# 128 bytes of padding in SBUF ahead of the K and V buffers of a decode kernel

## The chip, the cores and the metric

One core of a Trainium2 chip. The metric is the device time of one execution in microseconds, as a median over the runs of a kernel. All runs told here are of the fast kind; a kernel's runs agree within about 0.5%, most within 0.3%. Each ran beside runs of the kernel before on the same chip, so a kernel is compared by its ratio to the runs beside it.

## The reference, cut to what matters

One decode step for 8 sequences: layer norm, Q projection, attention of 32 query heads over the last 2048 positions of an 8-head KV cache, output projection, residual, then a small gated-shift block whose shifts are zero for one token, so that only its MLP (W3, GELU, W4) is left.

```python
W = min(4096, max(256, Sk // 4))                 # 2048
q = (x @ wq).reshape(B, Sq, Hq, Dh)...           # 8 x 1 x 512 by 512 x 4096
k = jnp.repeat(k_cache[:, :, Sk - W:, :], rep, axis=1)
v = jnp.repeat(v_cache[:, :, Sk - W:, :], rep, axis=1)
p = softmax(einsum(q, k) * Dh ** -0.5);  o = einsum(p, v) @ wo
...
h2 = gelu(layernorm(x1) @ w3) @ w4
```

K and V are 33.5 MB each in bf16, wq and wo 4 MB each, w3 and w4 1.8 MB each: 79 MB are read, and little is computed on them.

## The kernel before

Tiles are allocated one after another inside a partition, in the order of the code. The ones that matter (cut; the remarks are added here):

```python
wbig = sb([128, KC * H * DH], dt.bfloat16, "wbig")     # wq, later wo
qblk = sb([128, B, G, H], dt.bfloat16, "qblk")
knat = sb([128, NK, NC * DH], dt.bfloat16, "knat")     # 15 K slots of 4096 bytes; later w3, w4
...
vnat = sb([128, NV, NC * DH], dt.bfloat16, "vnat")     # 16 V slots of 4096 bytes
kT_sb = sb([128, NKT, W], dt.bfloat16, "kT_sb")        # K transposed, written by ScalarE and VectorE
```

SyncE issues all transfers into one queue: x, wq, then K slots with V five items behind, then wo, w3, w4. Each K or V transfer is 512 KB, one contiguous row of 4096 bytes per partition:

```python
e.dma_start(
    knat[:, ks, :].rearrange("p (c d) -> p c d", c=NC),
    A_k_cache[b, g, W0:SK, :].rearrange("(p c) d -> p c d", c=NC),
).then_inc(sem_k[ks], 16)
```

TensorE transposes each K slot into PSUM, ScalarE and VectorE move the halves to kT_sb, and TensorE makes QK and, once per sequence after the softmax, PV.

Of the kernel before, what the change touches and what calls it, by code (L numbers as in the profile page):

```python
# [6 lines left out]
dt = mybir.dt  # L7
# [26 lines left out]
def bass_sequential_preLN__sliding_block_cached__mixer_s_mlp__decode_kernel(  # L34
# [23 lines left out]
    with es:  # L58
        sb = lambda shape, dtype, name: es.enter_context(nc.sbuf_tensor(name, shape, dtype))
# [22 lines left out]

        qblk = sb([128, B, G, H], dt.bfloat16, "qblk")

        knat = sb([128, NK, NC * DH], dt.bfloat16, "knat")
        W3_SLOT0, W4_SLOT0 = 4, 8
        SLOT_E = NC * DH
# [667 lines left out]
```

## Time and profile before

| | before |
|---|---|
| median time | 207.4 us |
| span in the profile | 205.6 us |
| flow in the middle of the stream | 408 GB/s |
| PE busy, granted clock | 78%, 0.82 |
| first and second part of W4 land at | 199.98 and 201.91 us |

The flow of the DMA queue is the row to watch: the queue is full from the second slice of 40 to the 38th, and the flow is flat from the fourth to the 33rd. The prediction shows the lines. That is the first of W4's two parts (the semaphore updates in the trace show both, at 199.98 and 201.91), and TensorE waits once more for the second:

```profile
201.95 0.95 PEld L689 LDWEIGHTS b<-knat,gT 128*8 128x8 bf16 x12 [0.46 <-DMA knat<-in_B_w_dram]
```

### The profile page before, as it was taken

To read this page: it belongs to the slowest core of one execution; us is meant where nothing else is said; L and a number is where in the kernel's file an instruction comes from. 1 tells how busy PE (TensorE), PEld (TensorE's weight loads), DVE (VectorE), ACT (ScalarE), POOL (GpSimd) and SP (SyncE) were. 2 spreads that over 40 slices of the span, in tenths; PEclk is the share of its full clock that TensorE was granted. 3 is DMA by queue.
4 is the path that set the end of the run, shared out by engine and by line. 5 is a ranking of instruction groups with operands and counts; after the bars stand their busy time and mean duration, and the time that the engine had idled before them with its cause. 6 is when DMAs were issued, how large, how long until landed. Compare 5 with 4: busy or idle time off the path is not lost.

```text
span 205.6 us, 6282 instructions
## 1 busy us (share of the span) xinstructions
PE 161.1 (78%) x2744; PEld 123.5 (60%) x2744; DVE 83.4 (41%) x197; ACT 81.8 (40%) x101; POOL 3.0 (1%) x13
## 2 busy tenths in 40 slices
PE   1039957799779977995899699698996698775645
PEld 0039745487548754873688468575884576565542
DVE  5103534624562356234454444347345253351120
ACT  3203846514641464145523561157145341350040
POOL 5000000000000000000000000000000000000000
PEclk9999997975997599769696969579969588885556
DMA  6999999999999999999999999999999999999980
GB/s 206 440 388 416 409 408 410 409 408 407 405 411 408 407 410 409 406 409 410 406 410 406 408 409 410 407 406 408 409 406 408 410 410 381 356 393 340 398 305 22
DMA packets 24250, 79.59 MB, mean 387 GB/s; under 512 B 2192, under 2 KB 6304, under 8 KB 24096
## 3 DMA queue, kind: packets, MB, share of 16 engines
q1 hardware_dynamic: 24224, 79.19, 97.9%
q8 instruction: 22, 0.36, 0.7%
q14 instruction: 4, 0.03, 0.0%
HBM read 79.18 MB, written 0.01 MB: 385 GB/s over the span
## 4 chain that ended last, share of the span: by engine, by line
DMA 54%; SPq 24%; PE 18%; issue 2%; DVE 0%
DMA knat<-in_A_k_cache_dram 48%; SPq L239 12%; PE kT_ps L385 10%; SPq L249 7%; DMA knat<-in_B_w_dram 6%; SPq L259 4%; PE misc L523 3%; PE S_ps L415 2%; PE b L689 2%; SPq L277 1%; PE b L470 0%; PE misc L443 0%; PE b L504 0%; PE misc L475 0%; DVE out_sb L699 0%
## 5 line engine op out<-in xcount | busy, mean ns | idle before, releaser
L396 ACT ACTIVATE kT_sb<-kT_ps 128x1024 bf16<-128x1024 bf16 x64 | 65.4, 1023 | 87.7 <-PE kT_ps L385 87.6
L385 PE MATMUL kT_ps<-ident_b,knat 128*128 128x128 bf16 x1024 | 84.6, 249 | 19.6 <-DMA knat<-in_A_k_cache_dram 18.6
L385 PEld LDWEIGHTS kT_ps<-ident_b,knat 128*128 128x128 bf16 x1024 | 72.4, 113 | 36.9 <-DMA knat<-in_A_k_cache_dram 27.8
L403 DVE COPY kT_sb<-kT_ps 128x1024 bf16<-128x1024 bf16 x64 | 44.2, 691 | 61.9 <-PE kT_ps L385 61.9
L523 PE MATMUL misc<-pT_sb,vnat 128*128 128x4 bf16 x1024 | 29.0, 165 | 3.1 <-issue 1.6
L523 PEld LDWEIGHTS misc<-pT_sb,vnat 128*128 128x128 bf16 x1024 | 27.4, 98 | 6.6 <-issue 4.2
L415 PE MATMUL S_ps<-kT_sb,qblk 128*32 128x512 bf16 x256 | 29.0, 446 | 0.3 <-DVE kT_sb L403 0.3
L415 PEld LDWEIGHTS S_ps<-kT_sb,qblk 128*32 128x32 bf16 x256 | 6.6, 95 | 8.8 <-issue 3.3
L357 PE MATMUL S_ps<-xlnT,wbig 128*128 128x8 bf16 x128 | 3.6, 168 | 6.5 <-DMA wbig<-in_A_wq_dram 6.5
L436 ACT ACTIVATE P_sb<-S_ps,negmcol 128x512 bf16<-128x512 f32 x8 | 5.5, 687 | 7.2 <-DVE negmcol L428 7.2
L533 DVE TENSOR_TENSOR prod_sb<-misc,w_sb 128x128 f32<-128x128 f32 x8 | 2.3, 292 | 14.7 <-PE misc L523 14.7
L509 DVE COPY w_sb<-b 128x128 f32<-128x128 f32 x8 | 2.3, 292 | 13.5 <-PE b L504 13.5
L357 PEld LDWEIGHTS S_ps<-xlnT,wbig 128*128 128x128 bf16 x128 | 3.5, 104 | 6.5 <-issue 6.5
L426 DVE TENSOR_REDUCE mcol<-S_ps 128x1 f32<-128x512 f32 x8 | 5.5, 682 | 0.6 <-PE S_ps L415 0.6
L581 ACT ACTIVATE std<-var,eps_t 128x8 f32<-128x8 f32 x1 | 0.3, 301 | 12.4 <-DVE var L632 12.4
L373 DVE TENSOR_SCALAR qblk<-S_ps 128x32 bf16<-128x32 f32 x8 | 0.9, 182 | 9.8 <-PE S_ps L357 9.8
L504 PE MATMUL b<-w_row,ones_row 1*128 1x128 f32 x16 | 4.7, 385 | 0.0
L460 ACT ACTIVATE a_row<-d_row 1x128 f32<-1x128 f32 x8 | 2.5, 306 | 5.7 <-DVE d_row L453 5.7
L443 PE MATMUL misc<-ident_f,mcol 128*1 128x128 f32 x16 | 3.8, 328 | 1.0 <-DVE negmcol L428 1.0
L599 PE MATMUL S_ps<-oT_all,wbig 128*128 128x8 bf16 x128 | 3.7, 168 | 0.7 <-DMA wbig<-in_A_wo_dram 0.7
L599 PEld LDWEIGHTS S_ps<-oT_all,wbig 128*128 128x128 bf16 x128 | 3.6, 104 | 0.8 <-DMA wbig<-in_A_wo_dram 0.8
L659 PE MATMUL misc<-uT,knat 128*128 128x8 bf16 x56 | 1.7, 168 | 2.7 <-DMA knat<-in_B_w_dram 2.7
(78 smaller groups left out, 70.0 us busy)
## 6 DMA issues: line engine op xcount, KB each, us to landing
knat<-in_A_k_cache_dram SPq DMA_DIRECT2D x64, 512.0 KB, 15.6
vnat<-in_A_v_cache_dram SPq DMA_DIRECT2D x64, 512.0 KB, 15.8
wbig<-in_A_wq_dram SPq DMA_DIRECT2D x1, 4096.0 KB, 12.3
wbig<-in_A_wo_dram SPq DMA_DIRECT2D x1, 2048.0 KB, 19.9
knat<-in_B_w_dram SPq DMA_DIRECT2D x1, 1792.0 KB, 12.3
wbig<-in_A_wo_dram SPq DMA_DIRECT2D x1, 1024.0 KB, 12.3
wbig<-in_A_wo_dram SPq DMA_DIRECT2D x2, 512.0 KB, 11.2
knat<-in_B_w_dram SPq DMA_DIRECT2D x1, 1024.0 KB, 12.8
```

Source lines behind the costliest of these rows:

```text
L239: e.dma_start(vnat[:, vs, :].rearrange("p (c d) -> p c d", c=NC), A_v_cache[b, g, W0:SK, :].rearrange("(p c) d -> p c d", c=NC),).then_inc ...
L249: e.dma_start(knat[:, ks, :].rearrange("p (c d) -> p c d", c=NC), A_k_cache[b, g, W0:SK, :].rearrange("(p c) d -> p c d", c=NC),).then_inc ...
L259: e.dma_start(wo_v[:, h0:h1, :], A_wo[h0 * 128:h1 * 128, :].rearrange("(h p) n -> p h n", p=128)).then_inc(sem_wo[j], 16)
L357: ins = e.matmul(S_ps[:, 0, h * B:(h + 1) * B], wq_v[:, kc, h * DH:(h + 1) * DH], xlnT[:, kc * B:(kc + 1) * B], start=(kc == 0), stop=(kc ...
L385: ins = e.matmul(buf[:, c * 128:(c + 1) * 128], knat[:, ks, c * DH:(c + 1) * DH], ident_b[:, :], is_transpose=True)
L396: e.activation(kT_sb[:, i % NKT, 0:W // 2], kT_ps[i % 2][:, 0:W // 2], ACT.Copy).then_inc(sem_Elo, 1)
L403: e.tensor_copy(kT_sb[:, i % NKT, W // 2:W], kT_ps[i % 2][:, W // 2:W]).then_inc(sem_Ehi, 1)
L415: ins = e.matmul(S_ps[32 * q:32 * (q + 1), b % 2, :], qblk[:, b, g, :], kT_sb[:, i % NKT, 512 * q:512 * (q + 1)], start=(g == 0), stop=(g ...
L426: ins = e.tensor_reduce(mcol[:, j:j + 1], S_ps[:, j, :], AX.X, ALU.max)
L436: e.activation(P_sb[:, j, :], S_ps[:, j, :], ACT.Exp, bias=negmcol[:, j:j + 1], scale=1.0, accum_out=lcol[:, j:j + 1]).then_inc(sem_exp, 1)
L523: ins = e.matmul(misc[:, OT4.start + q * H + R * g:OT4.start + q * H + R * (g + 1)], vnat[:, vs, c * DH:(c + 1) * DH], pT_sb[:, b % 2, c, ...
L599: ins = e.matmul(hT_ps[:, k * B:(k + 1) * B], wo_v[:, h, k * 128:(k + 1) * 128], oT_all[:, h, :], start=False, stop=(h == H - 1), skip_gro ...
```

## The change

The intent is that the rows written by the transfers of K, V and the weights in the same buffer begin on a boundary of 512 bytes inside the partition. The tile itself is used by nothing.

```diff
         qblk = sb([128, B, G, H], dt.bfloat16, "qblk")
 
+        pad = sb([128, 128], dt.uint8, "pad")
         knat = sb([128, NK, NC * DH], dt.bfloat16, "knat")
```

## The prediction

> **What bounds the kernel now.** I read the 40 slices first, because they say whether one resource is full from end to end. Slices are 205.6 / 40 = 5.14 us.

> ```profile
> PE   1039957799779977995899699698996698775645
> ...
> PEclk9999997975997599769696969579969588885556
> DMA  6999999999999999999999999999999999999980
> GB/s 206 440 388 416 409 408 410 409 408 407 405 411 408 407 410 409 406 409 410 406 410 406 408 409 410 407 406 408 409 406 408 410 410 381 356 393 340 398 305 22
> DMA packets 24250, 79.59 MB, mean 387 GB/s; under 512 B 2192, under 2 KB 6304, under 8 KB 24096
> q1 hardware_dynamic: 24224, 79.19, 97.9%
> ```

> The DMA row is 9 from the second slice to the 38th, and from slice 4 to slice 33 the rate is flat at 405 to 416 GB/s: a queue that never empties and runs at a rate of its own. PE is high but not full. The stretches by time say the same with numbers (columns: length, busy time of PE, PEld, DVE, ACT, POOL, then clock, DMA share, GB/s):

> ```profile
> 40.00:60.00 20.00, 17.42 (x297) 13.56 (x296) 9.12 (x21) 9.14 (x11) 0.00 (x0) 0.83 1.02 407
> 60.00:80.00 20.00, 17.33 (x296) 13.36 (x294) 9.02 (x22) 8.70 (x12) 0.00 (x0) 0.83 1.03 409
> 120.00:140.00 20.00, 18.37 (x296) 13.91 (x294) 8.82 (x20) 8.03 (x9) 0.00 (x0) 0.78 1.03 408
> 140.00:160.00 20.00, 16.54 (x292) 12.64 (x289) 10.10 (x23) 9.37 (x12) 0.00 (x0) 0.91 1.03 408
> ```

> PE has 8 to 17% to spare at the granted clock while the DMA engines have none. Then the chain that ended last, to see what sets the end:

> ```profile
> DMA 54%; SPq 24%; PE 18%; issue 2%; DVE 0%
> DMA knat<-in_A_k_cache_dram 48%; SPq L239 12%; PE kT_ps L385 10%; SPq L249 7%; DMA knat<-in_B_w_dram 6%; SPq L259 4%; PE misc L523 3%; PE S_ps L415 2%; PE b L689 2%; SPq L277 1%; PE b L470 0%; PE misc L443 0%; PE b L504 0%; PE misc L475 0%; DVE out_sb L699 0%
> ```

> and its last pieces in order of time:

> ```profile
> 185.09 2.06 SPq L277
> 187.19 12.79 DMA knat<-in_B_w_dram
> 199.98 0.14 issue
> 200.12 3.30 PE b L689 x28
> 203.44 0.41 DVE out_sb L699
> ```

> The last transfer, W4, lands at 199.98, and only some 5.6 us of work follows. So the time is: all bytes through one full DMA queue, plus a short tail. Whatever shortens or lengthens each packet moves the end; nothing else in this diff could.

> **Where the packets go.** K and V are 128 transfers with one row of 4096 bytes per partition: 16384 packets, 1024 on each of 16 engines. The allocation table of the compiled kernel before gives the starts inside a partition: wbig 20864, knat 57728, vnat 119168, each 384 above a multiple of 512, that is 128 above a multiple of 256. Slots are 4096 bytes and W3's rows 3584 (7 times 512), so every packet of K, V, W3 and W4 starts at that offset. x_sb starts at 18624 (192 above a multiple of 256), out_sb at 212736 (a multiple of 256).

> [...]

> [...] Flow of 408 GB/s over 16 engines is 25.5 GB/s each, and 4096 bytes at that take 160.6 ns[...]. The packet records give the commonest durations by size: 1024 bytes 46 ns, 2048 84, 3584 140, 4096 159, 32768 1213. [...] a fixed 8.3 ns[...], per packet whatever its size. That is all an alignment could hope to take away[...].

> **The change part by part.** It adds one tile that nothing reads or writes: no instruction, wait or transfer is added or removed. It moves knat and everything allocated after it by 128 bytes: knat and vnat start at multiples of 512. wbig lies ahead of the pad, so wq and wo keep their offset, although the words of the change speak of weights: of these only W3 and W4, which live in knat, move. out_sb goes from a multiple of 256 to 128 above one. The end of the allocation, 213760 plus 128, stays within the partition.

> Packets that move, per engine: K and V 1024, W3 512/16 = 32, W4 896/16 = 56, together 1112. Each ns off a packet is therefore 1.11 us off the full queue, 0.54% of the time. Two per cent needs 4.15/1.11 = 3.7 ns of the 8.3.

> Is any of the 8.3 ns due to the offset? There are two comparisons inside this trace. First, x's 1024 byte rows land in SBUF at 192 above a boundary, and the output's 1024 byte rows leave SBUF and land in HBM with both ends on one; both come one to an engine, with no traffic of their own behind them. The commonest duration is 44 ns for x (6 of 8 packets) and 44 ns for the output (4 of 8, the others longer). [...] Second, the 4 byte completion writes, which cross no boundary, take 9 ns[...]. Both say that the 8.3 ns belong to the packet, not to its address. I choose **no saving** as the main case: 0 x 1112 = 0 us, time 207.4. TensorE, ScalarE and VectorE read and write the moved tiles at offsets that were multiples of 64 bytes before and still are; I count nothing for them.

> **The rivals.**
> 1. [...] A misaligned 4096 byte row touches 17 blocks of 256, not 16; [...] Against it: it leaves nothing for the packet's own overhead, and the output's aligned 1024 bytes should take 37.6 ns, not 44. Worth 9.4 x 1.11 = 10.5 us of queue. PE, 104 to 110 us busy in 120 of the stretch 40 to 160, would then have little slack, and in the half-clock spells (120 to 140, where the chain was PE's) it would stop the slot releases; I estimate 70 to 90% realised: 198 to 200 us.
> 2. [...] Worth 5.2 us: about 202.2, or 203 if PE keeps a little.
> 3. [...] 1.3 us, 206.1, which counts as the same. The 2 ns between x's isolated 44 ns and wo's 46 leave room for this much.
> 4. The write side is not the limit at all, and the read of HBM, whose rows are aligned before and after, sets the pace. Then even a real saving on the write is hidden: 207.4.
> 5. Slower: only by chance of SBUF placement. Nothing in the profile speaks for it; the output's misaligned read is 8 packets.

> **Range and chances.** I give the main case with rivals 3 and 4 about 77%, rivals 1 and 2 together 22% (most of it to 2 or a part of it), slower 1%. The three times before span 0.3%. The middle of this is a little under the time before: 207.0 us, range 204.0 to 208.2.

> **What would show it.** Right: the flat rate stays at 407 to 410 GB/s, the commonest 4096 byte packet stays at 159 ns, W4 lands near 200 and PE keeps its idle time on K. If the flow rises to 420 and the packet falls to about 155 ns, rival 2 holds; near 435 and 150 ns, rival 1. A control lies inside the run: wo's 1024 byte packets do not move and should keep 46 ns in all cases. Flow up but the time not, with longer waits of the DMA queue for PE and a rate with dips, would mean that PE took the bound over. My step most likely to fail is the inference from isolated packets of x and the output to packets back to back in a full queue.

The fixed 8.3 ns of a packet and the sizes of the first two rivals follow from the commonest durations listed there, of the kernel before. From 46 ns at 1024 bytes to 1213 ns at 32768 a packet grows by (1213 - 46) / 124 = 9.41 ns for each 256 bytes, and 46 - 4 x 9.41 leaves 8.4 ns at no bytes; both are estimates. Rival 1 puts one more piece of 9.41 ns on each row that starts off a multiple of 256: 17 x 9.41 = 160.0 ns, close to the 160.6 of the flow, and 5, 9, 15 and 129 such pieces are 47, 85, 141 and 1214 ns, close to the records too, so the sizes alone cannot choose between it and a fixed cost. Rival 2 puts on it the 128 bytes ahead of the row's start, 4.7 ns. Rival 3 is a small cost per row; its 1.3 us were the author's estimate. No run had shown yet that a row pays for any of them.

## The result, and the profile after

| | before | after |
|---|---|---|
| median time, us | 207.4 (207.33 to 207.88) | 202.89 (202.86 to 202.97) |
| ratio | 1 | 0.9778, interval 0.9762 to 0.9795 |

A ratio is the mean time of one kernel's fast runs over that of the other's fast runs of the same rounds, so it is not quite the ratio of the two medians. The kernel is 2.2% faster: faster, where the prediction had put 77% on the same.

The slices of the kernel after, in the same rows as before:

```profile
PE   2029985999679977995899779797998499785655
DMA  6999999999999999999999999999999999999980
GB/s 210 417 405 421 416 417 418 416 421 416 417 416 420 418 415 418 416 418 420 415 419 416 417 420 418 418 412 421 415 417 419 417 421 400 368 400 347 408 331 24
DMA packets 24250, 79.59 MB, mean 396 GB/s; under 512 B 2192, under 2 KB 6304, under 8 KB 24096
q1 hardware_dynamic: 24224, 79.19, 98.1%
```

The packet count and the bytes are the same, the queue is full as before, but the flow is 417 where it was 408. Nothing was removed; the same packets go faster. In the stretches that were shown of before:

```profile
40.00:60.00 20.00, 16.92 (x300) 13.11 (x298) 9.78 (x23) 9.17 (x11) 0.00 (x0) 0.91 1.02 417
60.00:80.00 20.00, 17.31 (x302) 12.99 (x300) 9.50 (x22) 9.17 (x11) 0.00 (x0) 0.91 1.03 418
120.00:140.00 20.00, 16.79 (x299) 12.98 (x297) 9.37 (x22) 9.04 (x12) 0.00 (x0) 0.91 1.03 417
140.00:160.00 20.00, 16.36 (x283) 12.75 (x280) 9.27 (x21) 8.49 (x11) 0.00 (x0) 0.83 1.03 417
```

The granted clock differs too (0.91 against 0.78 to 0.83 in three of the four). It is not the cause: a version below with the same gain ran at a mean clock of 0.818, the clock of the kernel before.

The chain that ended last says how the 4.5 us are spread. Its pieces from the second issue of the three later parts of wo, before (the rest is in the prediction; columns are start, length, what):

```profile
178.15 5.41 SPq L259
183.56 0.04 issue
183.61 1.44 SPq L259
```

and after, down to the end:

```profile
174.37 5.14 SPq L260
...
179.56 1.40 SPq L260
...
181.00 2.01 SPq L278
...
183.06 12.47 DMA knat<-in_B_w_dram
195.52 0.14 issue
195.66 3.17 PE b L690 x28
...
198.85 0.41 DVE out_sb L700
```

The wait for the second part of W4, after:

```profile
197.44 0.95 PEld L690 LDWEIGHTS b<-knat,gT 128*8 128x8 bf16 x12 [0.42 <-DMA knat<-in_B_w_dram]
```

At the start of this part the kernel after is already 178.15 - 174.37 = 3.78 us ahead. The packet records place the gain: the first packet of wo starts 3.28 us earlier (170.63 against 167.35), queued behind all but the last four V transfers; the last V packet ends 4.08 us earlier, the last packet of wo 4.17, and the second part of W4 lands 4.51 earlier (201.91 against 197.40). So most of the gain is the K and V stream, and some 1 us comes with the weights.

A K or V packet (one row of 4096 bytes, moved by one of the 16 engines) took 4096 x 16 / 408 = 160.6 ns of an engine's time before and 4096 x 16 / 417 = 157.2 after, if all bytes are put down to K and V. But the flow holds 15 packets of two other queues too (0.22 MB from 60 to 160 us). Counting the K and V packets alone in that stretch, 9911 and 10135, gives 161.4 and 157.9 ns: 3.6 ns less, and 1024 of them on an engine are 3.7 us. Taking off the 13.8 and 12.2 us that the records of the other 15 last leaves 160.0 and 156.7 ns. This is called the engine time per packet below, and is worked out in the same way for the other runs; it is an estimate from the traces, and the 4 byte packet that each transfer adds on an engine (commonest duration 9 ns) is in it.

The packet records of the two traces (no view prints them; they were counted) show how a packet changed. The duration of a record is longer than the engine time, because neighbouring records of an engine overlap by some 3.5 ns (in the kernel after a packet of 159 ns is followed 155.6 ns from its start by the next inside a transfer):

| 4096 byte packets | commonest | mean | share at 159 ns, 60 to 160 us |
|---|---|---|---|
| before | 159 ns | 163.1 ns | 0.40 |
| after | 159 ns | 159.9 ns | 0.996 |

The commonest duration did not move. What went away are the others: before, most of the packets took 160 to 172 ns. Put in their order on each engine (the records name no engine; ends were matched to starts), they come in repeating patterns of eight, such as 168, 159, 159, 165, 167, 159, 162, 164 over the eight rows of one transfer, and the same patterns return on other engines.

When the stalls begin is telling as well. At the start of the stream both kernels run alike. Before:

```profile
14.00:18.00 4.00, 4.00 (x129) 4.00 (x127) 0.79 (x8) 0.00 (x0) 0.00 (x0) 1.00 1.03 420
24.00:40.00 16.00, 11.89 (x152) 8.35 (x148) 6.82 (x13) 9.80 (x12) 0.00 (x0) 0.89 1.03 409
```

After:

```profile
14.00:18.00 4.00, 4.00 (x129) 4.00 (x126) 0.81 (x8) 0.00 (x0) 0.00 (x0) 1.00 1.03 420
24.00:40.00 16.00, 12.85 (x165) 9.07 (x163) 7.25 (x14) 10.37 (x12) 0.00 (x0) 0.89 1.03 417
```

From 14 to 18 us all 4096 byte packets of both kernels took 159 ns, misaligned or not. In the kernel before the first slow packet starts at 18.13 us, and on most engines they come at about 18.8 us, near the end of the fifth K transfer, after some 39 packets. Two readings fit. At that time ScalarE and VectorE begin to write kT_sb (at 18.08 and 18.94 us), so the stall could be a collision with the engines (theory C; the first expectations below call it theory A). Or the misaligned rows cost time by themselves, whatever the engines do, and the cost shows only after these 39 packets (theory W). Theory B is that the moved working tiles (kT_sb and later) count and not the transfers.

### The profile page after: what moved, and what is told of

The parts are those of the page before. It is cut to its first block, busy times and chain, and to the rows that moved or that the text cites.

```text
span 201.0 us, 6282 instructions
## 1 busy us (share of the span) xinstructions
PE 156.6 (78%) x2744; PEld 120.9 (60%) x2744; DVE 83.5 (42%) x197; ACT 81.9 (41%) x101; POOL 3.0 (1%) x13
## 2 busy tenths in 40 slices
DMA  6999999999999999999999999999999999999980
DMA packets 24250, 79.59 MB, mean 396 GB/s; under 512 B 2192, under 2 KB 6304, under 8 KB 24096
## 3 DMA queue, kind: packets, MB, share of 16 engines
q1 hardware_dynamic: 24224, 79.19, 98.1%
## 4 chain that ended last, share of the span: by engine, by line
DMA 60%; SPq 24%; PE 14%; issue 1%; DVE 0%
DMA knat<-in_A_k_cache_dram 53%; SPq L240 13%; PE kT_ps L386 7%; DMA knat<-in_B_w_dram 6%; SPq L250 6%; SPq L260 4%; PE misc L524 2%; PE b L690 2%; PE S_ps L416 1%; SPq L278 1%; PE b L471 1%; PE misc L476 1%; PE misc L444 0%; PE b L505 0%; DVE out_sb L700 0%
## 5 line engine op out<-in xcount | busy, mean ns | idle before, releaser
L386 PE MATMUL kT_ps<-ident_b,knat 128*128 128x128 bf16 x1024 | 81.4, 244 | 20.1 <-DMA knat<-in_A_k_cache_dram 20.1
L386 PEld LDWEIGHTS kT_ps<-ident_b,knat 128*128 128x128 bf16 x1024 | 69.9, 111 | 36.1 <-DMA knat<-in_A_k_cache_dram 29.3
L416 PE MATMUL S_ps<-kT_sb,qblk 128*32 128x512 bf16 x256 | 28.3, 425 | 0.4 <-DVE kT_sb L404 0.3
L471 PE MATMUL b<-ident_b,P_sb 128*128 128x128 bf16 x32 | 3.4, 232 | 0.4 <-ACT P_sb L437 0.4
## 6 DMA issues: line engine op xcount, KB each, us to landing
wbig<-in_A_wq_dram SPq DMA_DIRECT2D x1, 4096.0 KB, 12.3
```

The costliest lines, as they stand in the source:

```text
L386: ins = e.matmul(buf[:, c * 128:(c + 1) * 128], knat[:, ks, c * DH:(c + 1) * DH], ident_b[:, :], is_transpose=True)
L416: ins = e.matmul(S_ps[32 * q:32 * (q + 1), b % 2, :], qblk[:, b, g, :], kT_sb[:, i % NKT, 512 * q:512 * (q + 1)], start=(g == 0), stop=(g ...
```

## The experiments

The check of the result passed for every kernel, also for the pair with light engine work, which leaves out most of the attention on purpose; how much the check would let pass was not looked into. Flow is from 60 to 160 us of the profile. At a threshold of 2%, kv_only, off256, all_tiles and light_al count as faster, half_mis as slower, k_only as unclear and the others as the same; but the ratios of v_odd (0.9878 to 0.9911), light_mis (0.9952 to 0.9978) and half_al (1.0052 to 1.0091) lie clear of 1 too.

| kernel | offset of K, V above 256 | median us | ratio to before | flow GB/s | mean 4096 byte packet |
|---|---|---|---|---|---|
| kv_only | 0, 0, later tiles as before | 202.95 | 0.9784 | 417 | 159.8 ns |
| rest_only | 128, 128, later tiles moved | 207.47 | 1.0001 | 408 | 163.2 ns |
| off256 | 0, 0 (256 above 512) | 202.72 | 0.9774 | 417 | 159.9 ns |
| all_tiles | 0, 0, and wbig 0 | 202.72 | 0.9773 | 417 | 160.0 ns |
| off64 | 64, 64 | 207.75 | 1.0016 | 407 | 163.4 ns |
| off192 | 192, 192 | 207.65 | 1.0013 | 408 | 163.4 ns |
| k_only | 0, 128 | 203.35 | 0.9813 | 417 | 159.9 ns |
| v_odd | 128, 0 and 128 in turn | 205.19 | 0.9895 | 414 | 161.1 ns |
| light_mis | 128, 128 | 206.52 | 0.9965 | 409 | 163.1 ns |
| light_al | 0, 0 | 202.01 | 0.9745 | 419 | 159.5 ns |
| half_mis | 128, 128, rows of 2048 | 217.14 | 1.0465 | 386 | |
| half_al | 0, 0, rows of 2048 | 208.84 | 1.0071 | 403 | |

### Which tiles, and which boundary

**kv_only** moves K and V alone (with W3 and W4, which lie in K's slots); a second pad undoes the shift for what follows.

```diff
+        pad = sb([128, 128], dt.uint8, "pad")
         knat = sb(...)
         ...
+        pad2 = sb([128, 384], dt.uint8, "pad2")
         kT_sb = sb(...)
```

> K and V buffers start on a multiple of 512; a second pad of 384 bytes behind them puts all later tiles (kT_sb, P_sb and so on) back at the offset they had before. Theory A (a DMA write into a row that starts off a 256 byte boundary is stalled by engine accesses at the same time): full gain, 202.9 us, mean 4096 byte packet 159.9 ns. Theory B (the moved working tiles of the engines are what counts): no gain, 207.4 us, 163 ns.

202.95 us and 159.8 ns: the full gain, at a mean clock of 0.818.

```profile
60.00:160.00 100.00, 87.04 (x1464) 67.30 (x1462) 45.87 (x101) 44.49 (x53) 0.00 (x0) 0.82 1.03 417
```

**rest_only** has the pad ahead of kT_sb and none ahead of K.

```diff
         vnat = sb(...)
+        pad = sb([128, 128], dt.uint8, "pad")
         kT_sb = sb(...)
```

> The pad stands behind V, so only kT_sb and all later tiles move; K and V keep their offset. Theory A: 207.4 us, mean 4096 byte packet 163 ns. Theory B: 202.9 us, 160 ns.

```profile
60.00:160.00 100.00, 84.90 (x1454) 65.36 (x1452) 45.86 (x102) 43.10 (x52) 0.00 (x0) 0.86 1.03 408
```

207.47 us, 163.2 ns: nothing. Theory B is out; what counts is where the transfers' rows begin (or where PE reads them, which the light pair settles).

**off256** has a pad of 384 bytes.

```diff
+        pad = sb([128, 384], dt.uint8, "pad")
         knat = sb(...)
```

> Pad of 384 in place of 128 bytes: K and V start 256 above a multiple of 512. If 256 is the boundary that counts: 202.9 us, the same as the changed kernel. If 512 is needed: near 207.4 us, or between the two.

202.72 us: 256 is enough, although the words of the change say 512.

**all_tiles** puts the pad one tile earlier, so that wq and wo are on the boundary as well.

```diff
+        pad = sb([128, 128], dt.uint8, "pad")
         wbig = sb(...)
```

> The pad ahead of wbig, so that wq and wo are aligned as well. Theory A: wo's 4096 packets of 1024 bytes, mean 47.9 ns with wbig off the boundary, fall to 46 to 46.5, 257 packets on an engine: 0.4 us less than the changed kernel, 202.5 us. Theory B: the same as the changed kernel, 202.9 us.

Of wo's packets nearly all now take 46 ns (4031 of the 4112 packets of 1024 bytes, 3351 in the kernel after), mean 47.0 in place of 47.9. The time does not show it: 0.9773 against 0.9778 for the changed kernel, and 0.9784 and 0.9774 for kv_only and off256, whose wbig is off the boundary, all inside each other's intervals. No version here is clearly faster than the change.

### What a misaligned row costs

**off64** and **off192** ask how the cost depends on the offset: whether it is the same for every row that starts off the boundary (theory W1), or grows with the bytes between the boundary below and the start (W2).

```diff
+        pad = sb([128, 192], dt.uint8, "pad")     # off64;  64 in off192
         knat = sb(...)
```

> Pad of 192 bytes: K and V start 64 above a multiple of 256. Theory W1 ([...]17 slots in place of 16 at any offset): as the kernel before, 207.4 us, mean 4096 byte packet 163 ns. Theory W2 (only the bytes between the boundary below and the start are lost[...]): no longer the limit, 203 us.

> Pad of 64 bytes: K and V start 192 above a multiple of 256. W1: 207.4 us, 163 ns, as at 128. W2: [...]slower than before: about 209.6 us, 165 ns.

**half_mis** and **half_al** double the number of rows for the same bytes.

```diff
-                e.dma_start(knat[:, ks, :]..., A_k_cache[b, g, W0:SK, :]...).then_inc(sem_k[ks], 16)
+                for c0 in (0, NC // 2):
+                    e.dma_start(knat[:, ks, :]...[:, c0:c0 + NC // 2, :],
+                                A_k_cache[b, g, W0:SK, :]...[:, c0:c0 + NC // 2, :]).then_inc(sem_k[ks], 16)
...                                                          # V likewise; the waits count 32 per slot
```

> Offsets as before, but each K and V transfer cut into two, each with rows of 2048 bytes: 2048 packets of 2048 bytes on an engine in place of 1024 of 4096. Cost per row (9 touched blocks of 9.4 ns are 84.7 ns, against 80.0 from start to start for an aligned packet of this size): 3.3 to 4.7 ns a packet, so the time with aligned rows plus 7 to 9.5 us; about 217 us in all. Cost per byte: aligned plus 4.5 us.

> The same with the pad of 128 bytes. 1024 more packets of about 5 ns overhead and 128 more completion writes on an engine: about 209 us; below its misaligned twin by 7 to 9.5 us if the cost is per row, by 4.5 us if it is per byte.

217.14 against 208.84: 8.3 us, within the 7 to 9.5 of a cost per row and far from 4.5. The stretch from 60 to 160 us, misaligned:

```profile
60.00:160.00 100.00, 82.93 (x1396) 63.55 (x1392) 43.77 (x99) 40.60 (x49) 0.00 (x0) 0.84 1.05 386
```

and aligned:

```profile
60.00:160.00 100.00, 86.48 (x1452) 66.68 (x1448) 45.31 (x100) 43.26 (x51) 0.00 (x0) 0.85 1.05 403
```

At 386 GB/s a 2048 byte packet takes 2048 x 16 / 386 = 84.9 ns, and its engine time, without the other queues, is 84.7; 9 blocks of 9.41 ns are 84.7. The block count thus gives the misaligned engine time at two row lengths. The aligned engine time, 81.1 ns, is not 8 blocks (75.3): there something else is the limit. Two of them are 2 x 81.1 - 156.7 = 5.5 ns more than one aligned packet of 4096 bytes, where the expectation had about 5. These two lengths alone would fit a fixed cost per misaligned row as well; the mixed queues below tell the two apart.

### Engines or transfers

**light_mis** and **light_al** keep every transfer and cut the engines' work from the third sequence on; the result is wrong.

```diff
-            for c in range(NC):
+            for c in (range(NC) if i < 2 * G else (NC // 2 - 1, NC - 1)):          # transposes: 2 of 16
...
+            lo = 0 if i < 2 * G else W // 2 - 128                               # copies to kT_sb: 128 of 1024 columns
...
+            n = 512 if i < 2 * G else 64                                        # QK: 64 of 512 columns
...
-                    for jt in range(4):
+                    for jt in (range(4) if i < 2 * G else (0, 3)):              # PV: half
```

> Offsets as before, but from batch 2 on the engines do a fraction of their work (2 of 16 transposes, 128 of 1024 columns moved by ScalarE and VectorE, 64 of 512 columns in QK, half of PV); the result is wrong on purpose, all transfers stay. Theory W (the misaligned write costs by itself): the flow stays at 408 GB/s and the packet at 163 ns in the light stretch, 207 us. Theory C (the misaligned write collides with the engines' accesses): 417 GB/s, 159.5 ns, 203 to 204 us.

> The kernel with the engines' work cut, now with the pad of 128 bytes. If the engines have no part in the gain it is as large here as with full work: the time falls from 206.5 to about 202, the flow rises from 409 to 417 GB/s, the packet falls from 163 to 159.5 ns.

The stretch from 60 to 160 us of light_mis, then of light_al:

```profile
60.00:160.00 100.00, 41.90 (x661) 24.45 (x662) 27.80 (x101) 15.89 (x53) 0.00 (x0) 0.50 1.03 409
```

```profile
60.00:160.00 100.00, 43.53 (x674) 24.95 (x672) 27.73 (x103) 16.53 (x55) 0.00 (x0) 0.50 1.03 419
```

With PE's busy time halved, at half clock, and ScalarE's down to about a third, the misaligned flow is still 409 and the packet 163.1 ns; the pad alone brings 206.52 to 202.01, again 4.5 us (on two chips; the ratios to the kernel before are 0.9965 and 0.9745, 2.2% apart). Theory C falls: the engines have no visible part in the gain. The light kernels are each 0.7 to 0.9 us faster than their twins with full work, but in this stretch they also have 8 packets of other queues in place of 15; their engine time per packet is 160.1 and 156.3 ns, close to 160.0 and 156.7. A count in the trace of before points the same way: over the whole stream, with neither ScalarE nor VectorE busy in the middle of a packet, 46% of the 4096 byte packets took 161 ns or more, with ScalarE at its copy 51%.

### Two limits in series

**k_only** and **v_odd** mix aligned and misaligned packets in one queue.

```diff
+        pad = sb([128, 128], dt.uint8, "pad")                  # k_only
         knat = sb(...)
+        pad2 = sb([128, 384], dt.uint8, "pad2")
         vnat = sb(...)
```

```diff
-        vnat = sb([128, NV, NC * DH], dt.bfloat16, "vnat")     # v_odd: slots 4224 bytes apart
+        vnat = sb([128, NV, NC * DH + 64], dt.bfloat16, "vnat")
...
-                    vnat[:, vs, :]...
+                    vnat[:, vs, 0:NC * DH]...
```

> K (and W3, W4 in the same buffer) on the boundary, V and all else at the offset before. A cost of each misaligned packet by itself: half of the gain, 205.2 us, with half of the packets at 159 ns. A cost that needs K and V both misaligned (or a place where they meet): 203 us.

> V's slots 128 bytes further apart, so that every second V slot, a quarter of the K and V packets, is on the boundary. Two limits in series[...] (write side 160.0 ns misaligned, 150.6 aligned, mean 157.65 for this mix; packet limit 157.0 in the flow): most of the gain but not all, 2.6 of 4.5 us, about 204.8 us and 414 GB/s. Each packet for itself: a quarter of the gain, 206.3 us.

The stretch from 60 to 160 us of k_only, then of v_odd:

```profile
60.00:160.00 100.00, 84.80 (x1465) 65.51 (x1462) 45.87 (x102) 44.57 (x54) 0.00 (x0) 0.86 1.03 417
```

```profile
60.00:160.00 100.00, 83.82 (x1452) 64.95 (x1453) 45.24 (x101) 43.60 (x52) 0.00 (x0) 0.87 1.03 414
```

With half of the packets aligned, k_only has 4.0 of the 4.5 us, and nearly all packets, the misaligned V's too, take 159 ns. With a quarter aligned, v_odd has 2.2 us, half of the gain, at 414 GB/s (2.6 expected of two limits, 1.1 of each packet for itself). So the packets do not pay one by one. The k_only expectation of half the gain failed, and its other branch was worded as a need for both to be misaligned; the simpler reading is an average. If the limit that depends on the offset (the expectation calls it the write side) needs 160.0 ns for a misaligned row and, by the same count of blocks, 150.6 for an aligned one, both estimates, the mean is 155.3 for k_only's mix and 157.65 for v_odd's. The other limit, 156.7 ns in the kernel after, is above the first mean and hides it, and is just below the second: the engine time per packet is 156.7 in k_only and 157.9 in v_odd. Turned round, v_odd's 157.9 gives (157.9 - 0.75 x 160.0) x 4 = 151.6 ns for an aligned row under the first limit, an estimate that is near 16 blocks. A fixed cost of 160.0 - 156.7 = 3.3 ns for each misaligned row would have given 158.4 in k_only. The 0.4 us that k_only lacks come late: its first packet of wo starts at 167.32 us, as in the kernel after (167.35), and its last V packet ends at 183.07 in place of 182.52, in the stretch where misaligned V and misaligned wo rows follow each other. That fits an average over neighbouring rows; it was not tested by itself.

The beginning of the stream fits a limit that takes effect late: misaligned rows run at 420 GB/s for some 39 packets before they slow down. From start to start a packet of the kernel after takes 155.6 ns inside a transfer, 4.4 less than 160.0; times 39 that is about 170 ns, roughly one packet: an estimate, from these traces and the 160.0, of how far the rows get ahead of the slower rate before it shows. What lets them get ahead was not shown. The two limits and the count of blocks are a reading of rates; no record shows them directly.

What stays open: wo's packets have the same offset in both kernels, yet came shorter in the kernel after (mean 47.9 against 49.8 ns). They share the queue with the last V rows, and in k_only, where V is misaligned, the mean is 49.3 ns; but in light_al, where K and V are aligned, it is 49.6, so this is not all.

## Why the prediction was wrong

- **The bound** was right: one full queue, W4's landing and a short tail. Only the landing was misread: 199.98 us is the first part of W4, and after the second, at 201.91, there are 3.7 us of work, not 5.6. The gain arrived at the end undiminished; PE took nothing of it (the K slot waits of the queue rose, 12.3 to 20.4 us in total, but the chain's share for transfers rose as well, 54 to 60%).
- **What moves** was right: K, V, W3 and W4, 1112 packets on an engine, 1.11 us for each ns. With the 161.4 - 157.9 = 3.6 ns of the K and V packets that is 4.0 us of the 4.5. What it could not foresee is that wo's packets, which do not move, came 1.9 ns shorter, about 0.5 us for 257 on an engine.
- **The failed step** is "Both say that the 8.3 ns belong to the packet, not to its address. I choose no saving". The 8.3 ns come from the commonest duration, 159 ns, and that was right about what it measured: it is the same in every kernel here with rows of 4096 bytes. But the time is made of the mean. The mean of the same records was 163.1 ns, with 60% of the packets in the stream over 159, and the prediction did not ask why a flat stream of equal packets should have a long upper tail, nor why the first 549 of them had none. All of the gain on K and V lay in that tail. In place of no saving the runs show 3.6 ns a packet, with K and V alone (kv_only, 202.95 us) and not with the other tiles (rest_only, 207.47). An isolated packet of x or of the output could not show it: even in the full stream some 39 misaligned packets on an engine ran at 159 ns before the first slow one. The prediction named this inference as its most likely failure.
- **Rival 1** had the form of cost that the runs support (per row, nearly the same at offsets of 64, 128 and 192, in size near one more block) and a wrong size: 10.5 us, for it let the aligned row run at 150.6 ns. Its own objection, that it left nothing for the packet's overhead, assumed the two costs add. In the reading that the mixed queues support they do not add and the larger counts: 160.0 gives way to 156.7, not to 150.6.
- **Rival 2** came nearest in time, 202.2 us, by a count of the bytes ahead of a row's start, which off64 and off192 refute (207.75 and 207.65 us).
- **The control** inside the run was not one: wo's packets changed without being moved.

## What to carry to other kernels

When one full DMA queue sets the time, look at where each row lands inside its partition: here rows off a 256 byte boundary cost 2.2% with 4 KB rows and 4% (217.14 against 208.84) with 2 KB rows, and a dead tile cured it. Read the spread of equal transfers and not their commonest value: here a tail that began only some 6 us into the stream (first K packet at 12.57 us, slow packets on most engines at about 18.8) pointed to a second limit. Before sizing a gain, ask which limit comes next.
